# Where 1/sum is applied in an attention-and-Fourier kernel: to the weights by VectorE in place, instead of to the result through a transposition

## The chip, the cores and the metric

One Trainium2 chip, one of its cores. The metric is the device time in us of the whole program, and its profile is one execution taken by the hardware profiler. Engines: PE is TensorE, DVE is VectorE, ACT is ScalarE, POOL is GpSimd.

## The reference, cut to what matters

Eight batches of eight heads, 576 rows of 64, all fp32. Scores are thresholded a little under their row maximum, then softmax, then times v; the result is rearranged to 512 columns and goes through a Fourier mix and two matrix products.

```python
scores = scale * np.matmul(q, k.transpose(0, 1, 3, 2))
thresh = np.max(scores, axis=-1, keepdims=True) - tau
scores = np.where(scores >= thresh, scores, -1000000000.0)
attn = np.exp(scores - np.max(scores, axis=-1, keepdims=True))
attn = attn / (np.sum(attn, axis=-1, keepdims=True) + 1e-09)   # the division in question
x = np.matmul(attn, v)                                         # (B, H, S, D)
# ... x -> (B, S, 512); mixed = Re(FFT2(x)); u = x + mixed; normalise u;
# out = u + relu(un @ w1) @ w2
```

## The kernel before

Heads are worked in 32 pairs, four pairs a batch. A pair has five steps: four of 128 query rows for both heads, and one with the last 64 rows of both. Each step makes scores, a softmax without the division, and transposes the weights e so that they can be contracted with v. The sums lie along partitions of e (one per query row), but x comes out with query rows along its free dimension. So 1/sum is spread by POOL to a 128x128 tile, transposed by PE with the weights, and multiplied into x.

```python
def softmax(i, ...):                       # step i
    ...                                    # DVE: maximum; ACT: exp; DVE: threshold, sum -> den
    nc.vector.reciprocal(den[:, 0:nh], den[:, 0:nh])
    rec = sb.tile([128, 2 * D], FP32, tag="rec", name="rec")
    nc.gpsimd.tensor_copy(rec[...], _repeated(den[:, 0:nh], 2 * D // nh))
    if t == 4:
        nc.scalar.copy(e[:, S : S + 64], e[:, 512:S])

def transposed_weights(i):
    ...
    nc.tensor.transpose(pe[:, 0, :], e[:, 512:640], ident[:, :])
    nc.tensor.transpose(pe[:, 1, :], rec[:, :], ident[:, :])
    nc.scalar.copy(ends[:, :, qs], pe[:, 0:2, :])
    ...                                    # eight transpositions of e into pw, copied to e_t by ACT

def weighted_values(n):                    # pair n
    ...                                    # pv = v x e_t
    nc.vector.tensor_tensor(out=x[:, cols], in0=pv[:, 0:HALF], in1=ends[:, 1, cols], op=ALU.mult)
```

In the first two batches every engine's order is written by hand. From the third on (step 40 of 160) only PE's is, and a scheduler orders the others. The loop there:

```python
for i in range(2 * per_batch, total + 1):
    scores(i); softmax(i)
    fill()                                 # part of the Fourier mix or the matrix products (ph, po)
    transposed_weights(i - 1)
    if t == 3: prep_pair(n + 1)            # transposes the next q and k: pq, pk, pt
    fill(); fill()
    if t == 0: weighted_values(n - 1); ...
```

`prep_pair`: PE transposes q into the PSUM tile pq, and DVE moves it to qT (L390), which frees its bank. All small PE results share four banks: pe and pw (weights transposed), pq, pk and pt (q, k and their last rows transposed), pv (times v), py and pa (Fourier mix), pn (u transposed), ph and po (the two matrix products). The scores sc have their own.

## Time and profile before

| | before |
|---|---|
| time, three runs (a fourth came with the result) | 1766.71 us median, 1761.93 to 1766.92 |
| span of the profiled run | 1765.2 us |
| busy: PE, DVE, ACT, POOL | 98%, 44%, 37%, 20% |
| in 306 to 1545 us: PE busy | 1230.96 of 1239 us |

Busy shares tell which engine has least room. Where one engine has nearly none, as PE here, a change is worth what it takes from that engine's own stream, plus or minus the waits that it takes or brings.

### The profile page before, as it was taken

The page shows a single profiled execution, that of the slowest core. Times are in us where ns is not written, and L with a number is a line of the kernel's source. Part 1 is how long each engine was busy: PE and PEld are TensorE (multiplying, and loading weights), DVE is VectorE, ACT ScalarE, POOL GpSimd, SP SyncE. Part 2 cuts the span into 40 slices and gives each one's busy share as a digit, 9 for nine tenths or more (in the row PEclk, how much of TensorE's full clock was granted, in tenths as well). Part 3 has the DMA queues.
Part 4 walks back from the last instruction along what each step waited for, and adds up shares of the span by engine and source line. Part 5 has one row for each costly group of instructions (what it writes and reads, how often), then busy time and mean ns, then how long its engine had stood idle before and what let it go on. Part 6 is the DMA issues. An engine that isn't in the chain of part 4 may idle for free.

```text
span 1765.2 us, 21695 instructions
## 1 busy us (share of the span) xinstructions
PE 1722.5 (98%) x7892; PEld 992.8 (56%) x7892; DVE 769.6 (44%) x1955; ACT 657.3 (37%) x1462; POOL 347.2 (20%) x619
## 2 busy tenths in 40 slices
PE   8988989999999999999999999999999999999999
PEld 4555655555565556566555656556556556555453
DVE  6786765433344445433333544534324445421010
ACT  5774664323243344334223434433224334411010
POOL 5575542030110311021110212012101031110000
PEclk9999999999999999999999999999999999999999
DMA  5331311100100101010010110100001010000000
GB/s 157 106 99 57 99 54 37 33 14 14 32 18 23 27 20 30 24 32 15 12 34 14 27 33 21 28 26 23 11 26 28 23 29 8 1 12 6 12 6 18
DMA packets 130353, 57.03 MB, mean 32 GB/s; under 512 B 121124, under 2 KB 121126, under 8 KB 130247
## 3 DMA queue, kind: packets, MB, share of 16 engines
q1 hardware_dynamic: 128854, 55.35, 11.7%
q8 instruction: 63, 1.03, 0.2%
q10 hardware_dynamic: 1392, 0.30, 0.1%
q14 instruction: 44, 0.35, 0.1%
HBM read 46.02 MB, written 9.44 MB: 31 GB/s over the span
## 4 chain that ended last, share of the span: by engine, by line
PE 84%; DVE 7%; ACT 5%; POOL 1%; DMA 1%; issue 1%; SPq 1%; ACTq 0%; DVEq 0%; POOLq 0%
PE ph L725 27%; PE po L746 27%; PE pv L538 9%; PE sc L415 7%; PE pw L517 5%; DVE e L459 2%; PE sc L426 2%; ACT e L451 1%; DVE neg L443 1%; PE py L634 1%; PE pa L651 1%; PE pa L655 1%; PE pn L709 1%; PE pe L503 1%; PE pe L504 1%
## 5 line engine op out<-in xcount | busy, mean ns | idle before, releaser
L725 PE MATMUL ph<-u_t,w 128*128 128x384 f32 x1536 | 523.6, 491 | 2.1 <-ACT ends L507 1.2
L746 PE MATMUL po<-w,h 128*128 128x512 f32 x1152 | 524.4, 597 | 0.0
L451 ACT ACTIVATE e<-sc,neg 128x576 f32<-128x576 f32 x288 | 211.5, 734 | 504.5 <-DVE neg L443 503.5
L725 PEld LDWEIGHTS ph<-u_t,w 128*128 128x128 f32 x1536 | 283.1, 191 | 189.4 <-issue 14.8
L746 PEld LDWEIGHTS po<-w,h 128*128 128x128 f32 x1152 | 207.9, 190 | 221.4 <-issue 220.1
L443 DVE TENSOR_REDUCE neg<-sc 128x1 f32<-128x576 f32 x288 | 205.8, 751 | 283.8 <-PE sc L415 198.6
L459 DVE SCALAR_TENSOR_TENSOR e<-sc,thr,e 128x576 f32<-128x576 f32 x288 | 227.5, 815 | 92.0 <-ACT thr L455 88.9
L473 POOL COPY rec<-den 128x128 f32<-128x128 f32 x160 | 49.3, 308 | 1028.4 <-DVE den L471 687.6
L415 PE MATMUL sc<-kT,qT 64*128 64x288 f32 x1024 | 167.0, 434 | 4.5 <-DVE e L459 3.8
L517 PE MATMUL pw<-ident,e 128*128 128x128 f32 x1152 | 156.9, 276 | 12.7 <-ACT kT L395 5.8
L731 ACT ACTIVATE h<-ph 128x384 f32<-128x384 f32 x96 | 47.0, 490 | 267.2 <-PE ph L725 267.2
L519 ACT COPY e_t<-pw 128x512 f32<-128x512 f32 x256 | 139.8, 592 | 6.3 <-PE pw L517 3.0
L517 PEld LDWEIGHTS pw<-ident,e 128*128 128x128 f32 x1152 | 131.7, 142 | 16.9 <-ACT kT L395 6.7
L415 PEld LDWEIGHTS sc<-kT,qT 64*128 64x128 f32 x1024 | 92.4, 188 | 84.1 <-issue 60.1
L733 DVE TENSOR_SCALAR h<-ph 128x384 f32<-128x384 f32 x96 | 53.2, 555 | 185.1 <-PE ph L725 184.2
L543 DVE TENSOR_TENSOR x<-pv,ends 128x288 f32<-128x288 f32 x64 | 29.0, 456 | 173.2 <-PE pv L538 173.2
L753 DVE SCALAR_TENSOR_TENSOR u<-po,rstd,u 128x512 f32<-128x512 f32 x36 | 26.9, 748 | 139.3 <-PE po L746 139.2
L507 ACT COPY ends<-pe 128x256 f32<-128x256 f32 x128 | 47.6, 372 | 84.0 <-PE pe L504 77.0
L538 PE MATMUL pv<-e_t,v_rev 128*64 128x288 f32 x512 | 68.3, 409 | 0.6 <-ACT h L731 0.6
L538 PE MATMUL pv<-e_t,v_in 128*64 128x288 f32 x512 | 68.4, 409 | 0.0
L538 PEld LDWEIGHTS pv<-e_t,v_rev 128*64 128x64 f32 x512 | 35.3, 137 | 32.1 <-issue 6.2
L538 PEld LDWEIGHTS pv<-e_t,v_in 128*64 128x64 f32 x512 | 35.3, 137 | 32.0 <-issue 5.4
(145 smaller groups left out, 1532.5 us busy)
## 6 DMA issues: line engine op xcount, KB each, us to landing
stage<-in_moe_w_ch_dram SPq DMA_DIRECT2D x23, 512.0 KB, 4.0
out_dram<-u SPq DMA_DIRECT2D x36, 256.0 KB, 2.0
qk_in<-in_q_dram SPq DMA_DIRECT2D x64, 128.0 KB, 2.4
v_in<-in_v_dram SPq DMA_DIRECT2D x64, 128.0 KB, 2.4
w<-in_moe_w_ch_dram SPq DMA_DIRECT2D x9, 512.0 KB, 3.4
qk_in<-in_k_dram SPq DMA_DIRECT2D x31, 128.0 KB, 2.4
qk_in<-in_k_dram SPq DMA_DIRECT2D x31, 64.0 KB, 2.3
qk_in<-in_k_dram SPq DMA_DIRECT2D x93, 16.0 KB, 2.1
```

The lines of the kernel that those rows point to most:

```text
L415: nc.tensor.matmul(sc[j][:, c, 0:HALF], qT[hp, 128 * t : 128 * t + 128], kT[hp, HALF * c : HALF * (c + 1)], start=True, stop=True,)
L443: nc.vector.tensor_reduce(out=neg[:, j : j + 1], in_=sc[j][:, :, 0:HALF], axis=AXIS_XY, op=ALU.max, negate=True,)
L451: nc.scalar.activation(out=ej, in_=sc[j][:, :, 0:HALF], func=ACT.Exp, bias=neg[:, j : j + 1], scale=1.0)
L459: nc.vector.scalar_tensor_tensor(out=ej, in0=sc[j][:, :, 0:HALF], scalar=thr[:, j : j + 1], in1=ej, op0=ALU.is_ge, op1=ALU.mult, accum_out ...
L473: nc.gpsimd.tensor_copy(rec[:, :].rearrange("p (j d) -> p j d", j=nh), _repeated(den[:, 0:nh], 2 * D // nh))
L507: nc.scalar.copy(ends[:, :, qs], pe[:, 0:2, :])
L517: nc.tensor.transpose(pw[:, c, :], e[:, c0 : c0 + 128], ident[:, :])
L519: nc.scalar.copy(e_t[:, 4 * j : 4 * j + 4, qs], pw[:, :, :])
L538: nc.tensor.matmul(pv[64 * j : 64 * j + 64, 0:HALF], vt[:, 2 * c + j, :], e_t[:, 4 * j + c, cols] if c < 4 else ends[:, 0, cols], start=(c ...
L725: nc.tensor.matmul(ph[:, 0:GT], w1[c][:, 128 * j : 128 * (j + 1)], u_t[:, c, c0 : c0 + GT], start=(c == 0), stop=(c == ND - 1),)
L733: nc.vector.tensor_relu(ht, ph[:, 0:GT])
L746: nc.tensor.matmul(po[:, :], hT[j // 4][:, j % 4, 128 * t : 128 * (t + 1)], w2[j], start=(j == 0), stop=(j == NJ - 1),)
```

## The change

Its intent: PE is the bound, so take the 120 transpositions of 1/sum off PE from the third batch on, and multiply the weights by 1/sum on DVE, which is half idle. The product on x becomes a copy, and goes to ACT. The core of the diff (cuts marked):

```diff
+    def normalized(n):
+        return n >= 2 * NPAIR
 ...
         nc.vector.reciprocal(den[:, 0:nh], den[:, 0:nh])
-        rec = sb.tile([128, 2 * D], FP32, tag="rec", name="rec")
-        nc.gpsimd.tensor_copy(...)
+        rec = None
+        if normalized(i // NT):
+            for j in range(nh):
+                nc.vector.tensor_scalar(
+                    out=e[:, S * j : S * (j + 1)], in0=e[:, S * j : S * (j + 1)],
+                    scalar1=den[:, j : j + 1], scalar2=None, op0=ALU.mult,
+                )
+        else:
+            ...                            # rec as before
 ...
-        nc.tensor.transpose(pe[:, 1, :], rec[:, :], ident[:, :])
+        parts = 1
+        if rec is not None:
+            nc.tensor.transpose(pe[:, 1, :], rec[:, :], ident[:, :])
+            parts = 2
 ...
-            nc.scalar.copy(ends[:, :, qs], pe[:, 0:2, :])
+            nc.scalar.copy(ends[:, 0:parts, qs], pe[:, 0:parts, :])
 ...
-            nc.vector.tensor_tensor(
-                out=x[:, cols], in0=pv[:, 0:HALF], in1=ends[:, 1, cols], op=ALU.mult
-            )
+            if normalized(n):
+                nc.scalar.copy(x[:, cols], pv[:, 0:HALF])
+            else:
+                ...                        # the product as before
```

More of the change, by code (lines that the diff above doesn't have):

```diff
@@ L471, in softmax @@
         nc.vector.reciprocal(den[:, 0:nh], den[:, 0:nh])
-        rec = sb.tile([128, 2 * D], FP32, tag="rec", name="rec")
-        nc.gpsimd.tensor_copy(
-            rec[:, :].rearrange("p (j d) -> p j d", j=nh), _repeated(den[:, 0:nh], 2 * D // nh)
-        )
+        rec = None
[6 more added lines that the diff above has]
+        else:
+            rec = sb.tile([128, 2 * D], FP32, tag="rec", name="rec")
+            nc.gpsimd.tensor_copy(
+                rec[:, :].rearrange("p (j d) -> p j d", j=nh), _repeated(den[:, 0:nh], 2 * D // nh)
+            )
         if t == 4:
@@ L511, in transposed_weights @@
                 hp = slice(64 * j, 64 * j + 64)
-                nc.scalar.copy(ends[hp, :, qs], pe[hp, 0:2, hp])
+                nc.scalar.copy(ends[hp, 0:parts, qs], pe[hp, 0:parts, hp])
         for j in range(2 if t < 4 else 1):
@@ L542, in weighted_values @@
                     )
-            nc.vector.tensor_tensor(
-                out=x[:, cols], in0=pv[:, 0:HALF], in1=ends[:, 1, cols], op=ALU.mult
-            )
+            if normalized(n):
+                nc.scalar.copy(x[:, cols], pv[:, 0:HALF])
+            else:
+                nc.vector.tensor_tensor(
+                    out=x[:, cols], in0=pv[:, 0:HALF], in1=ends[:, 1, cols], op=ALU.mult
+                )
         if p % 2:
```

## The prediction

> **What bounds the kernel now.** I read the page from the top: the busy shares, then the table by stretches of the span, then what TensorE (PE) waited for, then the chain that ended last, and last the groups of instructions that the change touches. The page:
>
> ```profile
> PE 1722.5 (98%) x7892; PEld 992.8 (56%) x7892; DVE 769.6 (44%) x1955; ACT 657.3 (37%) x1462; POOL 347.2 (20%) x619
> ...
> PE 84%; DVE 7%; ACT 5%; POOL 1%; DMA 1%; issue 1%; SPq 1%; ACTq 0%; DVEq 0%; POOLq 0%
> ```
>
> The first line is busy us, share of the span, instructions; the second is the chain that ended last by engine. PE is the bound; VectorE (DVE) and ScalarE (ACT) are under half. But averages mix stages, so I cut the span. The change acts on pairs of heads 8 to 31, five steps each: 120 steps, from about 306 us (first reciprocal of that range) to 1545 us.
>
> ```profile
> 306.00:1545.00 1239.00, 1230.96 (x5804) 716.15 (x5804) 523.92 (x1369) 452.01 (x1019) 177.77 (x370) 1.00 0.09 22
> 1545.00:1765.00 220.00, 216.27 (x664) 112.69 (x662) 29.20 (x60) 18.86 (x55) 8.39 (x12) 1.00 0.03 11
> ```
>
> Columns: stretch, length, then busy us of PE, PE weight loads, DVE, ACT, POOL (GpSimd), granted clock, DMA share, GB/s. In the changed stretch PE is busy 1230.96 of 1239 us at full clock, so only 8 us are left in which anything else can be the limit; the tail after 1545 us is PE work too, and the change does not touch it. What those 8 us are, in the waits of PE in the stretch (us in total, times, longest):
>
> ```profile
> PE pt L396 <- ACT e_t L519: 2.5, 3, 0.8
> PE pw L517 <- ACT y_e L644: 1.2, 3, 0.4
> PE pa L651 <- ACT ends L512: 1.1, 6, 0.2
> PE py L634 <- DVE qT L390: 1.0, 4, 0.3
> ```
>
> No wait is for the row of 1/sum (rec) and none for the weights e. So the operation removed is worth only what it costs PE itself, and that is read from the chain, not from the busy time: the matmuls overlap.
>
> ```profile
> 1041.77 0.11 PE pe L503
> 1041.88 0.11 PE pe L504
> 1041.99 0.87 PE pw L517 x8
> ...
> 1060.67 0.11 PE pe L503
> 1060.78 0.11 PE pe L504
> 1060.89 0.87 PE pw L517 x8
> ```
>
> Columns: start us, us on the chain, what. L504 is the transposition of 1/sum, one per step. Its record lasts 0.27 us, but the next transposition starts 0.109 us after it: eight pw transpositions take 0.87 us.
>
> The groups concerned (out<-in, shapes, count | busy us, mean ns | idle before, releasers), first POOL's copies of 1/sum within the stretch, then lines of the whole span:
>
> ```profile
> L473 POOL COPY rec<-den 128x128 f32<-128x128 f32 x120 | 35.6, 296 | 928.0 <-DVE den L471 599.6 <-PE pe L504 100.1 <-PE pw L517 64.0
> ```
>
> ```profile
> L543 DVE TENSOR_TENSOR x<-pv,ends 128x288 f32<-128x288 f32 x64 | 29.0, 456 | 173.2 <-PE pv L538 173.2
> ```
>
> ```profile
> L507 ACT COPY ends<-pe 128x256 f32<-128x256 f32 x128 | 47.6, 372 | 84.0 <-PE pe L504 77.0 <-DVE x L543 6.6
> ...
> L666 ACT COPY tmp<-pa 128x289 f32<-128x289 f32 x16 | 6.3, 395 | 35.2 <-POOL u_t L673 21.1 <-PE pa L655 13.8 <-POOL u_t L677 0.3
> ```
>
> And one line of the whole-line view (minimum/median/maximum ns), the nearest relative of the new multiplication:
>
> ```profile
> L293 DVE TENSOR_SCALAR stage<-stage x21: 422/511/1700, 16.2 to 234.5; 128x512 int32<-128x512 int32 x21
> ```
>
> **What the Trainium skill says.** Four places. (1) "VectorE: DVE Perf Modes", section "The perf-mode tier table (the rule you actually need)": a tensor_scalar on fp32 from SBUF to SBUF runs at two elements a cycle, any PSUM operand at one. The trace agrees in kind: the last line above, a one-source DVE operation of 512 32-bit elements within SBUF, has a minimum of 422 ns, while L443 takes 751 ns for 576 elements from PSUM. (2) "SBUF — State Buffer", section "Who interferes with whom": such a two-port operation and a GpSimd instruction exclude each other, the later one standing still until the other ends. The same line fits: median 511, maximum 1700 ns, in a stretch where POOL is over half busy. That is agreement, not proof. (3) "TensorE: Matmul & The Clock Gate", section "Part 4: PE-mode transpose", gives about 275 ns for a 128x128 transposition inside a kernel; L504's median record is 273 ns, so that agrees, but it is a duration, and the 109 ns between starts is what counts in a stream. (4) "Perfetto Trace Analysis", section "Identifying the Most-Contended Engine", warns that matmul busy time misleads because matmuls are pipelined. The weight loads are indeed only 56% busy; but the chain and the list of waits show PE held by its own stream, so I keep PE as the bound.
>
> **The change part by part.**
>
> PE: 120 transpositions go (the order of PE instructions is by hand, and is otherwise the same line for line). 120 x 0.109 = 13.1 us, all in a stretch where PE has 8 us of slack in 1239. On the path.
>
> POOL: 120 copies at 296 ns go, 35.6 us. Off the path; 177.8 - 35.6 = 142 us are left, 11.5% of the stretch.
>
> DVE added: in 96 steps two multiplications of 128x576, in 24 steps one: 216. L293 takes 422 ns for 512 elements undisturbed; 64 more at two a cycle of 0.96 GHz (the VectorE page's clock) are 33 ns, so I take 450 ns for 576 (estimate). 216 x 0.45 = 97 us. With POOL busy 11.5% and its instructions 0.5 to 1.5 us long, I expect one in seven to wait 0.4 us or so: 216 / 7 x 0.4 = 12 us. DVE removed: 48 products x at 456 ns, 22 us. Net +88 us: DVE 524 to about 612 us of 1239, 49%. Off the path unless one stands in front of something PE waits for.
>
> ACT added: 48 copies of 128x288 from PSUM at 394 ns (L666 is the same shape but for one column): 19 us. ACT removed: the copy from pe shrinks from 256 to 128 columns in 96 steps, 372 to about 270 ns (L715, 129 columns, has 281): 10 us; 48 half-size ones by about 50 ns: 2 us. Net +7 us; off the path, and the copies that free the PSUM banks of pw come 0.1 us earlier in 96 steps, which should take some tenths off the ACT waits above: -0.5 us.
>
> The longer chain: e is now ready after the reciprocal plus two multiplications, about 0.85 us later. From each step's reciprocal to its first transposition (L503) the trace has at least 1.99 us (at 692 us) and 9.1 us in the median of the 120 steps. So 1.1 us stay in the worst. The score banks are freed before the reciprocal, so the next scores don't wait for the multiplications.
>
> What may stand behind the multiplications: in the order of instructions, after them DVE comes to the next maximum (33 times of 120), to relu evacuations L733 (23), to the output's L753 (16), to the evacuation of the transposed q, L390 (13), and to others. L390 is the tender one: before, it often starts as soon as DVE is free of the reciprocal (7 of 15 without a gap), and PE waited for it four times already. 13 delays of 0.85 us, of which other banks absorb most, plus a few late L733: I put +2 us, between 0 and 8.
>
> Sum: 1766.7 - 13.1 - 0.5 + 2 = 1755 us, 0.7% less.
>
> **The rivals.**
>
> A: The multiplications take the place of the transposition as what PE waits for. For it: DVE is strictly in order, 0.85 us stand before L390 and L733, the POOL lock can stretch one to 1.5 us, and 22 of the 120 steps have under 4 us between reciprocal and L503. Against: DVE has half of each 10.3 us step to itself, and the waits of PE for DVE before come to 1.0 us in the whole stretch. If each of the 24 steps that prepare a pair lost 0.5 us and twenty L733 lost 0.4: +20 us, 1774.
>
> B: ACT becomes the limit, with x's copies in front of the copies that free pw and pk. For it: the largest PE waits are for ACT already. Against: its net load is +7 us, the x copies come once per five steps, right after the weighted values, and their fellow pe copies got shorter. At worst 24 x 0.2 = 5 us: 1760.
>
> C: Nothing is seen, because PE starved where the transposition stood and its slot was filler. For it: in the chain some L503 take 0.26 instead of 0.11. Against: that wait is on L503, which stays, and L504 takes 0.11 even there. It would give 1766.
>
> D: The gain is larger, as the record (0.27 us) or the weight load (0.14 us) counts: 120 x 0.27 = 32 us, 1734. Against: starts 0.109 us apart.
>
> **Range and chances.** The main term, 13.1, is a count times a spacing that repeats; the uncertainty is stalls of 0 to 8 us (to 20 in rival A) and the spread of the three runs before, 1761.9 to 1766.9. So 1755, with 1750 to 1762 eight times in ten. Two per cent faster is 1731, below even D: 1%. Two per cent slower is 1802, beyond A: 2%. Within 2%: 97%.
>
> **What would show each step.** PE instructions 7892 to 7772, the starts of pe and the first pw 0.109 us apart; PE still near 99% of the stretch, which ends about 11 us earlier. The multiplications near 450 ns with a tail over 1 us where POOL runs; over 700 ns in the median would mean one element a cycle, and DVE at 55%. PE's waits for DVE (qT, h) at 1 to 5 us in total; for e at nearly nothing. x copies near 394 ns, the pe copy near 270. The prediction is wrong if PE's waits in the stretch grow by over 8 us, whoever the releaser, or if the multiplications push L390 or L733 so that PE stops once in each pair.

## The result, and the profile after

1753.83 us median of four runs (1751.86 to 1757.4) against 1764.32 us of four runs of the kernel before (1761.91 to 1766.92). The ratio is 0.9943, with a 95% interval of 0.9917 to 0.9968: the same within 2%, about 0.6% faster. The prediction was 1755.

The page of the changed kernel, busy us and share and instructions, then its chain by engine:

```profile
PE 1707.7 (98%) x7772; PEld 978.5 (56%) x7772; DVE 858.9 (49%) x2123; ACT 662.3 (38%) x1510; POOL 317.1 (18%) x499
...
PE 83%; DVE 7%; ACT 5%; issue 3%; POOL 1%; DMA 1%; SPq 1%; ACTq 0%; DVEq 0%; POOLq 0%
```

PE has 120 instructions fewer, DVE 89 us more, ACT 5 us more, POOL 30 us less. The chain of the changed kernel (start us, us, what) shows the slot gone: pw starts 0.11 us after pe.

```profile
1031.37 0.11 PE pe L516
1031.48 0.87 PE pw L533 x8
```

**Spans of single runs mislead here.** The two profiled spans differ by 15.2 us (1765.2 and 1750.0), more than the runs do. A part of that has nothing to do with the change. Here is the stretch from 20 to 40 us of both profiles, before and then changed; both kernels execute the same instructions there. After the stretch and its length come the busy us of PE, weight loads, DVE, ACT, POOL, then the granted clock:

```profile
20.00:40.00 20.00, 17.24 (x88) 10.46 (x88) 16.35 (x42) 14.69 (x31) 9.97 (x12) 0.91 0.56 156
```

```profile
20.00:40.00 20.00, 16.80 (x93) 10.40 (x91) 16.98 (x45) 15.52 (x33) 10.10 (x13) 1.00 0.56 161
```

In the run before the clock was at 0.91 there, in the other at 1.00. From the first PE instruction to the start of step 40 the two runs took 314.5 and 309.3 us; another run below (transposition twice), whose first 40 steps are instruction for instruction those of the kernel before, took 309.0. So I measure in the stretch that the change touches: from the first transposition of step 40 to that of step 159, 119 steps, with the same hand-written PE order but for the transposition taken out. Before:

```profile
316.06 0.27 PE L503 MATMUL pe<-ident,e 128*128 128x128 f32 x1
...
1542.95 0.27 PE L503 MATMUL pe<-ident,e 128*128 128x128 f32 x1
```

Changed (the same line of code is L516):

```profile
310.86 0.27 PE L516 MATMUL pe<-ident,e 128*128 128x128 f32 x1
...
1527.91 0.27 PE L516 MATMUL pe<-ident,e 128*128 128x128 f32 x1
```

That is 1226.9 us before and 1217.1 us after: 9.8 us less. The tail after it is 222.2 and 222.1 us, and 222.1 to 222.3 in all the runs below; one program traced on two chips (by POOL in the preparing step only) took 1214.4 and 1214.3 us in the stretch. So differences of half a us count here. I then laid PE's common instructions of the stretch side by side, 5618 times from one start to the next, and added these up. The transpositions of 1/sum account for -12.99 us (119 x 0.109). The rest is +3.15 us of waits, in few places that recur with the schedule: after pn +2.3, after the scores +0.9, after pw +0.6, after pt +0.6, after ph and py +0.5 each, after pk -2.0, after pq -0.3. The question for the experiments is what these 3.1 us are.

PE's waits in the changed kernel, 310 to 1530 us (total us, times, longest), to be read against the list in the prediction:

```profile
PE py L653 <- ACT ends L523: 2.3, 3, 0.8
PE py L653 <- ACT kT L395: 2.1, 4, 0.5
PE pw L533 <- ACT tmp L685: 1.2, 3, 0.4
PE ph L744 <- POOL u_t L692: 1.1, 1, 1.1
PE ph L744 <- ACT e_t L535: 1.0, 3, 0.3
PE ph L744 <- DVE qT L390: 0.6, 2, 0.3
```

PE waits nowhere for the weights e, as predicted. The total is about the same (8.3 us here; the whole list before, of which the prediction shows four lines, comes to 7.8), but it moved: the four waits that the prediction shows are gone from the list, and others stand in their place. A wait for qT now stops ph, and one for kT stops py. Here is one such place. Before: the reciprocal ends, DVE waits for PE's pq and evacuates it at 816.22, and ph starts without a gap (start us, us, engine, line).

```profile
815.55 0.17 DVE L471 RECIPROCAL den<-den 128x2 f32<-128x2 f32 x1
...
816.22 0.75 DVE L390 TENSOR_SCALAR qT<-pq,q_scale 128x512 f32<-128x512 f32 x1 [0.51 <-PE pq L389]
...
816.57 0.60 PE L709 MATMUL pn<-ident,u_t 128*128 128x128 f32 x4
...
817.03 1.24 PE L725 MATMUL ph<-u_t,w 128*128 128x384 f32 x3
```

Changed: two multiplications stand between, so qT is done later, and ph waits for it. From the first pn to ph it is 0.46 us before and 0.89 us here.

```profile
806.17 0.17 DVE L476 RECIPROCAL den<-den 128x2 f32<-128x2 f32 x1
806.38 0.95 DVE L480 TENSOR_SCALAR e<-e,den 128x576 f32<-128x576 f32 x2
...
807.15 0.60 PE L728 MATMUL pn<-ident,u_t 128*128 128x128 f32 x4
807.24 0.74 DVE L390 TENSOR_SCALAR qT<-pq,q_scale 128x512 f32<-128x512 f32 x1
...
808.04 1.24 PE L744 MATMUL ph<-u_t,w 128*128 128x384 f32 x3 [0.29 <-DVE qT L390]
```

The new operations themselves (minimum/median/maximum ns):

```profile
L480 DVE TENSOR_SCALAR e<-e,den x216: 502/520/1716, 300.9 to 1524.8; 128x576 f32<-128x576 f32 x108
```

```profile
L560 ACT COPY x<-pv x48: 399/399/401, 369.6 to 1537.1; 128x288 f32<-128x288 f32 x48
```

Of the 216 multiplications, 191 ran while POOL did nothing and took 502 to 522 ns; of the 25 that met a POOL instruction 17 took more than 530 ns, up to 1716. One of the longest pairs of DVE, and the POOL instructions around it:

```profile
587.53 2.58 DVE L480 TENSOR_SCALAR e<-e,den 128x576 f32<-128x576 f32 x2
```

```profile
586.09 2.19 POOL L696 TENSOR_TENSOR u_t<-x,tmp 128x287 f32<-128x287 f32 x3
588.24 2.41 POOL L692 TENSOR_TENSOR u_t<-x,tmp 128x289 f32<-128x289 f32 x3
```

The pair takes 2.58 us where 0.95 is usual, and POOL goes from one instruction to the next through it: the record of the first multiplication, 1716 ns, spans the end of one POOL instruction, two whole ones and the start of a fourth.

### The profile page after: what moved, and what is told of

Its sections match the earlier page's. It is cut to its first block, busy times and chain, and to the rows that moved or that the text cites. A ratio compares the mean times of both kernels' runs of the same rounds, so it can differ in the third digit from the quotient of the medians.

```text
span 1750.0 us, 21426 instructions
## 1 busy us (share of the span) xinstructions
PE 1707.7 (98%) x7772; PEld 978.5 (56%) x7772; DVE 858.9 (49%) x2123; ACT 662.3 (38%) x1510; POOL 317.1 (18%) x499
## 4 chain that ended last, share of the span: by engine, by line
PE 83%; DVE 7%; ACT 5%; issue 3%; POOL 1%; DMA 1%; SPq 1%; ACTq 0%; DVEq 0%; POOLq 0%
PE ph L744 27%; PE po L765 27%; PE pv L554 8%; PE sc L420 7%; PE pw L533 5%; DVE e L464 2%; PE sc L431 2%; ACT e L456 1%; PE py L653 1%; DVE neg L448 1%; PE pa L670 1%; PE pa L674 1%; PE pe L516 1%; PE pn L728 1%; PE pm L355 1%
## 5 line engine op out<-in xcount | busy, mean ns | idle before, releaser
L585 POOL TENSOR_TENSOR half<-x 128x287 f32<-128x287 f32 x48 | 40.3, 859 | 542.2 <-ACT x L560 239.0
L692 POOL TENSOR_TENSOR u_t<-x,tmp 128x289 f32<-128x289 f32 (+1 forms) x47 | 36.4, 783 | 540.2 <-DVE tmp L689 539.8
L480 DVE TENSOR_SCALAR e<-e,den 128x576 f32<-128x576 f32 x216 | 115.5, 572 | 3.4
L560 ACT COPY x<-pv 128x288 f32<-128x288 f32 x48 | 19.2, 399 | 149.9 <-PE pv L554 133.8
L523 ACT COPY ends<-pe 128x128 f32<-128x128 f32 (+1 forms) x128 | 37.2, 291 | 71.1 <-PE pe L516 62.9
```

Source lines behind the costliest of these rows:

```text
L480: nc.vector.tensor_scalar(out=e[:, S * j : S * (j + 1)], in0=e[:, S * j : S * (j + 1)], scalar1=den[:, j : j + 1], scalar2=None, op0=ALU.mult,
```

## The experiments

All are judged by the stretch of 119 steps: 1226.9 us before, 1217.1 us changed. Steps before 40 are those of the kernel before except where said.

| run | stretch us | time us |
|---|---|---|
| before (profiled run) | 1226.9 | 1764.32, median of 4 |
| changed (profiled run) | 1217.1 | 1753.83, median of 4 |
| transposition alone away | 1214.5 | 1751.05 |
| transposition twice | 1240.0 | 1774.71 |
| multiplications alone added | 1231.7 | 1769.16 |
| multiplications later in the program | 1218.0 | 1753.69 |
| x copied by DVE | 1217.4 | 1754.14 |
| multiplications by POOL | 1245.9 | 1783.28 |
| second head by a constant, half width in each fifth step (wrong result) | 1216.6 | 1755.11 |
| by POOL in the preparing step only | 1214.4 | 1751.48; timed again 1750.58 |
| the same, from the second batch | 1214.2 | 1753.02 |
| changed, from the first pair | 1216.8 | 1773.94 |

**What is one transposition worth?** Away alone (wrong result: x is multiplied by another row):

```diff
-        nc.tensor.transpose(pe[:, 1, :], rec[:, :], ident[:, :])
+        parts = 1
+        if i < 2 * NPAIR * NT:
+            nc.tensor.transpose(pe[:, 1, :], rec[:, :], ident[:, :])
+            parts = 2
```

> The kernel before with the transposition of 1/sum left out from the third batch on and nothing else changed (GpSimd still spreads 1/sum, VectorE still multiplies x, but by another row of the same tile, so the result is wrong on purpose; ScalarE's copy of pe is narrower, as in the change). Measured in the stretch from the first transposition of step 40 to that of step 159 (119 steps; 1226.9 us before, 1217.1 us changed). Theory of the slot (109 ns each): 1226.9 - 13.0 = 1213.9 us, give or take 0.5. Rival C (the transposition filled idle time): 1226.9. Rival D (its 273 ns record counts): 1194. If the multiplications cost the missing 3.1 us, this run has 1213.9; if leaving out the transposition itself brings the new waits of ScalarE, it has 1217.

And twice:

```diff
+        if i >= 2 * NPAIR * NT:
+            nc.tensor.transpose(pe[:, 2, :], rec[:, :], ident[:, :])
```

> The kernel before with the transposition of 1/sum made twice from the third batch on, the second into an unused quarter of the same bank, never read; right result. Slot theory: stretch 1226.9 + 13.0 = 1239.9 us, give or take 0.5. Rival C: 1226.9. Rival D: 1259.

Measured: 1214.5 and 1240.0 us. The slot of 109 ns holds in both directions, 12.4 us off and 13.1 us on; neither idle filler (0) nor the record's 273 ns (32) fits. The first run keeps 0.6 us of new waits although it has no multiplication, so that much comes with a stream that is otherwise timed. At four places PE waits for qT after pt both before and in this run, and there the slot is not gained: the gap grows from 0.58 to 0.69 us, by as much as the transposition took. Elsewhere two gaps after pk and pt, in one preparation of every second batch, shrink by 0.9 us together and the one after pn grows by 0.5, in this run as in the changed kernel.

**Do the multiplications cost PE anything?** Added alone (wrong: divided twice):

```diff
+        if i >= 2 * NPAIR * NT:
+            for j in range(nh):
+                nc.vector.tensor_scalar(... e *= den[:, j : j + 1] ...)
```

> The kernel before with the multiplications of e added from the third batch on, while 1/sum is still spread by GpSimd, transposed and multiplied into x (so the result is divided twice by the sum: wrong on purpose). If the multiplications in VectorE's queue cost PE the missing 3.1 us by themselves: stretch 1229 to 1231 us. If they are hidden: 1226.9 within 0.5. Multiplications: 0.52 us where GpSimd is idle; GpSimd now starts the copy of 1/sum right after the same reciprocal, so if the two exclude each other, many more than 25 of the 216 are lengthened, by up to 0.3 us.

Measured: 1231.7 us, 4.8 more than before and above the range expected. So they do, though DVE is half idle. It is also more than the 2.6 us between the run without transposition and the changed kernel: 0.7 us are two gaps in which pk waits for DVE's evacuation of the output (u, L753 of the kernel before), which the changed kernel doesn't show; for the rest of the difference I have no account. The part about exclusion came out on both sides. 202 of the 216 multiplications now met a POOL instruction, and 100 took more than 530 ns (17 in the changed kernel), but 81 of these only 540 to 560; the median was 0.52 us as before. The first of a pair started before POOL's copy of 1/sum, and the copy stood still. The copy's mean went from 296 ns (shown in the prediction) to 534:

```profile
L473 POOL COPY rec<-den 128x128 f32<-128x128 f32 x119 | 63.5, 534 | 902.9 <-DVE den L471 620.9 <-PE pe L510 97.4 <-PE pw L523 47.9
```

Which of the two waits depends on which began first; that they exclude each other is seen from both sides.

**Is it their place in DVE's queue?** First try: emit them after the preparation of the next pair.

```diff
-            for j in range(nh): nc.vector.tensor_scalar(... e *= ...)    # in softmax
+            weights[i] = (e, den, nh)
 ...
             prep_pair(n + 1)
+        multiplied(i)                                                     # here instead
         fill()
```

> The changed kernel with the multiplications (and the small copy behind them in the fifth step) placed later in the program, after the preparation of the next pair, so that VectorE comes to the evacuation of q (qT) first. If the missing 3.1 us are waits of PE for qT behind the multiplications: stretch 1214 to 1215.5 us, the gaps of 0.49 and 0.43 us after pn gone. If they are ScalarE's reordering: they stay, 1216.5 to 1217.5 us.

Measured: 1218.0 us, nothing gained. The trace tells why the experiment doesn't answer: the scheduler still put the multiplications ahead of qT (at the place shown above both, 0.95 us; at another one of the two), because DVE's order is not the program's here. The gap after pt even grew, from 0.84 to 1.18 us, four times; why is told below.

Second try: take them out of DVE's queue just where qT follows, with POOL doing them in that one step of each pair.

```diff
-                nc.vector.tensor_scalar(
+                (nc.gpsimd if i % NT == 3 else nc.vector).tensor_scalar(
```

> The changed kernel with the multiplications done by GpSimd only in the step of each pair in which the next pair is prepared (24 steps), so that nothing new stands ahead of the evacuation of q; right result. If that evacuation is one cause: the gaps after pt (0.84 us, four times) back to 0.58 or less and after pn (0.56, three times) back to 0.13, stretch 1217.1 - 4 x 0.26 - 3 x 0.43 = 1214.8 us, give or take 0.7. If it is not: 1217.

Measured: 1214.4 us, 2.7 less than the changed kernel. At the place shown above, qT waits only for PE again and ph follows without a gap, while POOL works beside:

```profile
807.64 0.17 DVE L476 RECIPROCAL den<-den 128x2 f32<-128x2 f32 x1
...
807.97 3.43 POOL L480 TENSOR_SCALAR e<-e,den 128x576 f32<-128x576 f32 x2 [16.45 <-DVE den L476]
...
808.27 0.75 DVE L390 TENSOR_SCALAR qT<-pq,q_scale 128x512 f32<-128x512 f32 x1 [0.47 <-PE pq L389]
...
809.07 1.88 PE L744 MATMUL ph<-u_t,w 128*128 128x384 f32 x5
```

The gap after pn went from 0.56 back to 0.13 us in two places and stayed in the others, those that the run without multiplications has too; after pt it went from 0.84 to 0.62, four times; some smaller ones went with them. The sum is 2.7 us, and what is left over the ideal (1213.9) is 0.5 us, about the 0.6 of the run without any multiplication. So the multiplications that DVE makes in the preparing steps cost 2.7 of the 3.15 us. 0.9 of it is after pn, where the lines show qT behind them; 0.9 is after pt; the rest are smaller gaps, most of them after pw, whose way I did not follow.

How the gap after pt comes about can be read from the traces. The changed kernel at one of the four places (start us, us, engine, line):

```profile
570.62 0.32 PE L396 MATMUL pt<-ident,qk_in 128*128 128x128 f32 x1
570.82 0.59 ACT L395 COPY kT<-pk 128x512 f32<-128x512 f32 x1 [0.26 <-PE pk L394]
571.43 0.75 DVE L390 TENSOR_SCALAR qT<-pq,q_scale 128x512 f32<-128x512 f32 x1
571.45 0.94 PE L653 MATMUL py<-dim_c,f 128*128 128x65 f32 x6 [0.52 <-ACT kT L395]
```

At these four places py starts 0.05 us after the end of one of two copies in the seven runs that I compared. In the kernel before it is qT, which ends 0.53 us after pt's start. In the changed kernel qT ends 1.56 us after it, behind the multiplications, and py follows kT instead, at 0.79. With the multiplications later in the program py followed qT again, which was late by one multiplication (1.13 us): hence the longer gap there. With POOL in this step it follows qT, at 0.56. That py takes the bank which that copy frees, and that the scheduler chose which, is a reading of these waits; the trace does not name banks.

**All by POOL?**

```diff
-                nc.vector.tensor_scalar(
+                nc.gpsimd.tensor_scalar(
```

> The changed kernel with all multiplications by GpSimd; right result. If the missing 3.1 us come from multiplications standing in VectorE's queue: stretch near that of the run without transposition and multiplication, 1214 to 1215.5 us, with e ready about 1 us later and GpSimd busy 150 to 200 us more. If GpSimd then delays the rows of u and the folds that PE needs: over 1217.

Measured: 1245.9 us. That is over 1217, as the second theory had it, but far over, since I had POOL's multiplication too short. It takes 1722 ns in the median, and now PE waits not only for the rows of u but for e itself, which neither theory named:

```profile
PE pe L516 <- POOL e L480: 12.6, 10, 2.5
PE ph L744 <- POOL u_t L692: 8.9, 3, 4.1
```

This shows where the slack between reciprocal and first transposition (at least 1.99 us before) ends: two multiplications of 0.52 us fit, two of 1.72 us don't.

**Are ACT's copies of x part of it?**

```diff
-                nc.scalar.copy(x[:, cols], pv[:, 0:HALF])
+                nc.vector.tensor_copy(x[:, cols], pv[:, 0:HALF])
```

> The changed kernel with x copied out of PSUM by VectorE instead of ScalarE; right result. If the copies of x in ScalarE's queue are part of the missing 3.1 us (rival B): stretch 1215 to 1216.5 us. If they are hidden: 1217.1 within 0.5; VectorE busy about 20 us more, ScalarE 19 us less.

Measured: 1217.4 us. No: they are hidden on either engine. Rival B falls.

**What sets the 520 ns?** The multiplication of the second head by a constant, and a half width in each fifth step (wrong):

```diff
-                    out=e[:, S * j : S * (j + 1)], in0=e[:, S * j : S * (j + 1)],
-                    scalar1=den[:, j : j + 1], ...
+                    out=e[:, S * j : S * j + w], in0=e[:, S * j : S * j + w],     # w = 576, or 288
+                    scalar1=0.5 if j else den[:, j : j + 1], ...
```

> The changed kernel as a measuring rod for the multiplication, wrong on purpose: of two heads the first is multiplied by its pointer scalar as before (576 elements), the second by a constant 0.5, and in each fifth step only 288 elements are multiplied by a pointer scalar. Where GpSimd is idle: first 0.517 us as before. If the pointer scalar costs the 47 ns that my estimate missed: second 0.45 to 0.48 us; if not: 0.517. Fifth step: 0.517 - 288/2/0.96 ns = 0.367 us at two elements a cycle, 0.217 us at one.

```profile
L481 DVE TENSOR_SCALAR e<-e,den x120: 369/520/1153, 304.6 to 1527.9; 128x576 f32<-128x576 f32 x96, 128x288 f32<-128x288 f32 x24
L481 DVE TENSOR_SCALAR e<-e x96: 444/450/2033, 304.1 to 1520.9; 128x576 f32<-128x576 f32 x96
```

With a constant it is 450 ns, exactly the estimate of the prediction; with the scalar read from memory the record is 70 ns longer. DVE's next instruction, where it follows at once, starts 365 ns after the start of the first kind and 429 ns after that of the second. Undisturbed, the half width took 371 ns in the median, so 288 elements are 149 ns: 0.52 ns each, which is two elements in a cycle of 0.96 GHz, the clock that the Trainium skill gives ("VectorE: DVE Perf Modes", section "Specifications").

**Could the change reach further back?** From the first pair on:

```diff
-        return n >= 2 * NPAIR
+        return True
```

> The changed kernel with the multiplications and without the transposition from the first pair on. From the first to the 20th step the kernels so far took 133.6 to 138.3 us, with the granted clock varying there, and VectorE and ScalarE bound it more than PE: each step has two multiplications of 0.52 us in VectorE's queue, 20 us in all, against 2.1 us of PE's slots. If VectorE binds in these steps: 145 to 158 us; if PE does: 132 to 136.

Measured: the steps 0 to 20 take 155.0 us, where the kernels so far took 132.3 to 138.3. There PE waits for DVE (0 to 310 us):

```profile
PE pw L533 <- DVE qT L390: 12.3, 3, 4.7
PE sc L420 <- DVE e L464: 8.1, 12, 3.0
PE sc L431 <- DVE e L464: 3.8, 3, 2.0
```

In the first 160 us the kernel before has DVE busy for 120, as DVE also takes part in converting the two weight matrices there (L290 to L306). The granted clock was 0.93 in these 160 us against 0.96 before, 3% less, where the 20 steps took 12% longer or more; so the clock alone is not the reason. So the limit "from the third batch on" is better than none. From the second batch on, together with POOL in the preparing step later, and that last version by itself, both timed in five rounds on one chip:

> The same with the multiplications and without the transposition from the second batch on (VectorE in all its steps there). If the transposition's slot counts there too and nothing waits: the 20 steps from step 20 to step 40 take 158.3 - 20 x 0.109 = 156.1 us, the kernel about 14.7 us under the one before, ratio 0.9917. If VectorE, 67 to 80% busy there, now makes PE wait: 158 to 162 us and nothing gained.

> The kernel with GpSimd multiplying in the preparing step only, timed in five rounds. Its stretch was 12.5 us under the kernel before (1226.9 - 1214.4); the rest of the span is the same program. So about 12.5 us under the kernel before, ratio 0.993, interval some 0.002 either way; the changed kernel's 9.8 us would be 0.9944, so times alone may not tell the two apart, the traces do.

Measured: the version with POOL in the preparing step has 1750.58 us (1749.09 to 1752.75) against 1763.93, ratio 0.9922, interval 0.991 to 0.9934; its stretch was 1214.3 again. It is the fastest of all, and beats both kernels, the changed one by 2.7 us in the stretch; the intervals of the two ratios against the kernel before overlap, so it is the traces that tell them apart. From the second batch on: ratio 0.9944, interval 0.9929 to 0.9958. Its steps 20 to 40 took 160.3 us where 156.1 was the hope and 158.2 to 159.2 the rule. Nothing is gained there, so the limit is well placed.

## Why the prediction was right, point by point

- PE's term, 120 x 0.109 = 13.1 us on the path: right. The trace has 12.99 us for the 119 steps of the stretch, and the runs with the transposition away and doubled give 12.4 and 13.1.
- Stalls of +2 us, by L390 behind the multiplications: right in kind and nearly in size; taking the preparing step's multiplications off DVE gave 2.7 us back. The sign that the prediction named for it did not come: PE's waits for DVE were to be 1 to 5 us and are 0.6 (before: 1.0). Only the gaps after pn show as waits for qT; after pt the late qT shows as a wait for ACT's kT. The relu evacuations (L733) and L753, which I had counted with it, do not appear in the changed kernel's list of waits; L753 does in the run with the multiplications added alone.
- The -0.5 us from earlier copies on ACT: it is there, and is outweighed. The six gaps in which pa waited for ACT's copy of pe are 0.105 us shorter each, 0.6 us, in the changed kernel and in the run without multiplications. But other waits for ACT came where listed ones went (6.1 us of them before, 6.6 changed), and in the run without multiplications the sum of all gaps stood at +0.6 us against the pure slot.
- Sum: 11.7 us predicted, 9.8 in the stretch, 10.5 by the medians. The missing 1 to 2 us are these last two terms. That 1755 came within 1.2 us of 1753.83 is in part luck: it started from a median of three runs that is 2.4 us above that of the four, and this made up for the saving put too high.
- DVE's load: +88 us predicted, 89.3 measured, with luck inside. A multiplication is 520 ns and not 450, because I took it from a relative that has constants where this one has a pointer; but the two of a step overlap by 0.08 us (0.95 for two of 0.517), 8 us in all, and they overlap with their neighbours by 4.2 us more, which I had not taken off. The collisions with POOL, put at 12 us, come to 11.9 us over 517 ns each, but as 17 of 0.70 us where I had 31 of 0.4.
- ACT +7 us: 5.0; the copy of x 399 ns for 394, the copy of pe 263 for 270. POOL -35.6: -30.1, because some of POOL's other instructions got longer, most of all the one-row additions of u (L692 of the changed kernel, 682 to 846 ns in the mean) and the fold's first additions (821 to 859 ns, over the span).
- e is late but not too late: right, PE never waits for it.
- Three readings in the prediction were loose, without weight in the sum. L443 (751 ns) is a reduction, another kind of operation than the multiplication; the like one from PSUM is L390, 744 ns for 512 elements. DVE's instruction after the 120 reciprocals, counted again, is L733 24 times, L443 21, L753 16 and L390 15 times. And the 275 ns that it quotes for a transposition are given there for bf16; this one is fp32.
- Rival A was the right mechanism at an eighth of its size (2.7 us for 20). B is refuted by moving the copies of x, C and D by the doubled transposition.

## What to carry to other kernels

When one engine is full and its order fixed, price an operation on it by the distance between starts in its stream, not by its record, and check the price by doubling the operation. Work moved to a half idle engine is not free: look at what stands behind it in that engine's queue and frees a buffer for the full one; here 2.7 of 13 us went back with the work of the preparing steps, and moving that, 24 of 120 steps, to a slower, idler engine recovered them. Where a start-up clock varies, compare a stretch in the traces and not whole spans.

## What the Trainium skill lacked or had wrong

- "VectorE: DVE Perf Modes", section "Scalar operands": says that the scalar may be a constant or a per-partition operand, not what the second costs. Here the record is 70 ns longer per instruction (450 against 520 ns at 576 fp32 elements within SBUF).
- "SBUF — State Buffer", section "Who interferes with whom": agrees that a two-port operation and GpSimd exclude each other, and that who begins first decides; the runs show it from both sides (POOL's copy 296 to 534 ns, the multiplication 520 to 1716 ns). What it doesn't say is whether DVE can wait through several GpSimd instructions in a row, not just the one that runs; the record of 1716 ns above spans two whole ones.
- "TensorE: Matmul & The Clock Gate", section "Part 4: PE-mode transpose": gives the duration (about 275 ns inside a kernel, for bf16; here 273 for fp32) but no rate in a stream. For fp32 128x128 it is 109 ns from start to start, and removing or doubling 120 of them moved the time by 12.4 and 13.1 us.
- "GPSIMD Engine Reference", section "4.1 Engine selection": says that GpSimd is about 2 times slower than VectorE for two inputs and "roughly line-rate" for one. Its multiplication of 128x576 fp32 by a per-partition scalar takes 1722 ns in the median, 3.3 times DVE's 520.
- "Perfetto Trace Analysis", section "Identifying the Most-Contended Engine": it judges PE's distance to its roofline by MFU (the share of the peak arithmetic rate) and by the busy share of weight loads. MFU was not worked out here. Weight loads were busy 56%, which alone would suggest room; yet 12.4 of the 13.0 us taken off PE's stream came back as time. For what one instruction on PE is worth, PE's waits have to be read beside it.
